# Hashed attention before a gated feed-forward block: the first batch's hash products taken pair by pair over four column groups, and its order of work rewritten

## The chip, the cores and the metric

The kernel runs on one core of a Trainium2 chip. The metric is device time in microseconds (us), the median of three runs: 339.31 us before the change (339.14 to 339.33). One more execution, taken with the hardware profiler, lasted 338.95 us; the span of its instructions, from the first to the last, is 337.2 us, and 1.75 us lie around it.

Engines are named as in the profile: PE is the matrix engine (PEld its weight loads), DVE the vector engine, ACT the activation engine, POOL the general engine, SP the engine that issues most transfers. Each works through its own list of instructions in order, and waits on semaphores where data come from another.

## The reference, cut to what matters

```python
q_bits = (einsum('bhsd,dk->bhsk', q, proj) > 0)     # 6 bits per token and head
k_bits = (einsum('bhsd,dk->bhsk', k, proj) > 0)
mask   = q_bucket[:, :, :, None] == k_bucket[:, :, None, :]
scores = where(mask, scale * q @ k.T, -1e9)
attn   = softmax(scores) @ v                        # batch 4, heads 8, 768 tokens, 64 dims
x      = attn, heads side by side                   # 3072 x 512
out    = x + sigmoid(x @ w_res) * ((gelu(x @ w_gate) * (x @ w_val)) @ w_out)
```

A token attends only to the tokens of its head whose six sign bits (a hash by `proj`) are the same. Everything that arrives is float32.

## The kernel before

**Pairs and batches.** Two heads form a pair; pairs 0 to 3 are batch 0, pairs 4 to 7 batch 1, and so on to pair 15. A tile that belongs to "(p, 0)" is of the q side of pair p, "(p, 1)" of its k side. The 768 tokens of a head lie on 128 partitions, six to a partition, so a pair's q has 12 blocks of 64 (`HT` = 12, `T` = 6).

**From q and k to scores.** `load` (L158) fetches one side of a pair, 384 KB, `load_v` (L166) its values; both are issued by SP and go through one queue, in order. `cast` writes q or k as bf16 into one of four tiles `nat`. `tr` (L270) turns the float32 blocks on DVE, 32x32 at a time, into `t32`. The hash product (L281) multiplies `t32` by `projw` in float32, two halves of the 64 dims summed, 32 output columns per job; up to four jobs stand side by side in four column groups of PE. DVE turns the sums back (`tokens`, L293), and `bits` (L302) writes the signs as six extra columns of `nat`, in four instructions of 32 partitions for a side, dealt out to DVE and POOL by a string such as 'vvvp'. With one more column of constants each token then has 71 columns, and one product of 71 rows gives the score and adds a large bonus for each equal bit. `turn` transposes `nat` on PE (L378) into PSUM and `copy` (L384 on ACT, L386 on DVE or POOL) brings it to `aug`; `turn_dma` (L364) does it by a transposing transfer instead, as for pair 3.

**Scores and values.** A pair has nine chunks. `S c` is chunk c of the batch (c = 0 to 35; pair 1 begins at S 9, pair 2 at S 18, pair 3 at S 27): PE fills 128x1024 scores into one of two PSUM buffers (L505), ACT takes the exponential (L516). `V c` multiplies the result by the values (L480). `vs` and `va` prepare the values of a pair on POOL (L391 to L403); `preset` adds a small share of `vs` to a head's sums on PE (L452, L455). `finish` (L424, L425) divides a head on DVE and writes `x_tok`; `xturn` (L464 to L469) or a transposing transfer (L433) makes `x_sb` of it, which the feed-forward products read.

**After the first batch.** `gate_val` multiplies `x_sb` by `wg` and `wv` (L530). Of its first step the parts of pairs 0 to 2 are done early (`gv` 0 and 1); the part of pair 3 waits for `finish` (3, 1) and `xturn` 3. Then come the hash products of pairs 6 and 7, which need `tr` (6, *) and `tr` (7, *). The later batches interleave scores with the feed-forward products of the batch before; their order comes from the lists in the kernel's body and isn't touched.

**What sets the order.** For batch 0 the order is written out by hand: `PLAN` (L17 to L73) is a list of steps, and each step puts its instructions at the end of its engine's list. Only the order within an engine counts; a load that stands late in PLAN is issued as soon as SP has come through what stands ahead of it. `('w',)` lets POOL issue the next piece of the weights (L245, 384 KB for each piece of `wg` and `wv`); the first two pieces stand in PLAN, seven more follow without a wait behind POOL's last step of PLAN. Buffers also order the work: four for each side's loads, three for `load_v`, one for the PSUM tile "r" (hash sums, and some `turn`s), one for the turned hash `ht`.

Before the change pair 1 is hashed by itself, both sides in two column groups (`hash (1,)`, eight matmuls), pairs 2 and 3 together in four (`hash (2, 3)`, sixteen matmuls).

## Time and profile before

| what | value |
|---|---|
| median of three runs | 339.31 us |
| the profiled execution, its span | 338.95 us, 337.2 us |
| PE busy | 331.5 us (98%) |
| DVE, ACT, POOL busy | 217.0, 213.3, 175.4 us |
| mean granted PE clock | 0.998 |
| bytes moved | 43.88 MB, 130 GB/s over the span |
| S 0 starts on PE, the last exponential of batch 0 starts on ACT | 7.70 us, 44.36 us |
| first product of the feed-forward block starts | 45.90 us |

A timeline row gives the start, the duration of the group, the engine, the line, the operation, the tiles (out<-in) with their shapes and the number of instructions merged into the row; in brackets stands the idle time just before, with what ended it. "PE busy" counts a matmul to its modelled end, so that consecutive rows of PE overlap a little; the chain of waits, where one piece begins when the one before ends, gives the time a group takes out of the sequence. A landing is counted from a transfer's issue to its semaphore.

### The profile page before, as it was taken

Reading aid. Unit: us, or ns where it says so; the run is one execution under the profiler, and the core shown is the slowest. Engines: PE = TensorE matmul, PEld = TensorE weight load, DVE = VectorE, ACT = ScalarE, POOL = GpSimd, SP = SyncE. Lnnn points to the kernel's source line nnn. Section 1 sums busy time; section 2 is a strip of 40 time slices with the busy share of each in tenths; the row PEclk is TensorE's granted clock in tenths of the full one; section 3 lists DMA queues with packets and bytes.
Section 4 is the critical chain, followed back from the end, with each engine's and each line's share of the span. In section 5 each row is a group of like instructions: output and inputs, shape, how many; then the busy total and the mean of one; then the engine's idle time right before and its main releaser. Section 6 shows DMA issues by size and latency. Waiting matters only on the chain.

```text
span 337.2 us, 7848 instructions
## 1 busy us (share of the span) xinstructions
PE 331.5 (98%) x3138; PEld 202.7 (60%) x3138; DVE 217.0 (64%) x461; ACT 213.3 (63%) x246; POOL 175.4 (52%) x261
## 2 busy tenths in 40 slices
PE   7999999999999999999999999999999999999996
PEld 6667666565666655655666665666566665666444
DVE  7887675664577958875687896876567444343243
...
GB/s 231 373 286 132 222 237 182 187 159 232 287 204 177 62 95 78 107 36 98 92 108 272 303 77 92 135 49 62 35 124 33 80 103 31 33 0 0 33 62 94
DMA packets 74387, 43.88 MB, mean 130 GB/s; under 512 B 52544, under 2 KB 71360, under 8 KB 74352
## 3 DMA queue, kind: packets, MB, share of 16 engines
q1 hardware_dynamic: 67872, 37.95, 44.4%
...
HBM read 29.56 MB, written 6.29 MB: 106 GB/s over the span
## 4 chain that ended last, share of the span: by engine, by line
PE 93%; ACT 3%; DVE 2%; issue 1%; DVEq 0%; ACTq 0%
PE sp L530 37%; PE fps L576 18%; PE sp L505 17%; PE av L480 9%; PE rps L562 6%; PE hs L281 3%; ACT ering L516 3%; PE wps L226 1%; ACT e L516 1%; PE hs L319 1%; PE pt L378 1%; PE pt L464 0%; DVE nat L329 0%; DVE o L582 0%; DVE aug L386 0%
## 5 line engine op out<-in xcount | busy, mean ns | idle before, releaser
L516 ACT ACTIVATE e<-sp 128x1024 bf16<-128x1024 f32 x117 | 117.7, 1028 | 8.3 <-PE sp L505 3.2
L339 POOL TENSOR_TENSOR pr<-ld,projr 128x384 f32<-128x384 f32 x96 | 93.8, 998 | 48.2 <-DVE sums L345 29.0
L547 ACT ACTIVATE gt<-sp 128x768 bf16<-128x768 f32 x48 | 38.9, 810 | 83.5 <-PE sp L530 77.9
L505 PE MATMUL sp<-aug,aug 71*128 71x256 bf16 (+1 forms) x384 | 86.2, 326 | 0.4
L576 PE MATMUL fps<-wo,hh 128*128 128x512 bf16 (+2 forms) x312 | 79.6, 363 | 0.0
L550 DVE TENSOR_TENSOR hh<-gt,sp 128x768 bf16<-128x768 bf16 x48 | 45.8, 954 | 44.2 <-PE sp L530 40.8
L530 PE MATMUL sp<-x_sb,wv 128*128 128x512 bf16 (+1 forms) x384 | 70.9, 326 | 0.0
L530 PE MATMUL sp<-x_sb,wg 128*128 128x512 bf16 (+1 forms) x384 | 70.9, 326 | 0.0
L480 PEld LDWEIGHTS <-e 128*128 128x128 bf16 x936 | 43.5, 97 | 25.9
L345 DVE TENSOR_REDUCE sums<-pr 128x6 f32<-128x384 f32 x96 | 50.0, 541 | 11.6 <-POOL pr L339 11.0
L530 PEld LDWEIGHTS <-wg 128*128 128x128 bf16 x384 | 37.0, 98 | 25.6 <-issue 1.2
L530 PEld LDWEIGHTS <-wv 128*128 128x128 bf16 x384 | 37.4, 98 | 25.0 <-issue 0.2
L480 PE MATMUL av<-va,e 128*128 128x65 bf16 x936 | 47.1, 193 | 0.0
L576 PEld LDWEIGHTS <-hh 128*128 128x128 bf16 x312 | 28.1, 97 | 22.0 <-issue 0.2
L505 PEld LDWEIGHTS <-aug 71*128 71x128 bf16 x384 | 29.0, 97 | 11.5 <-issue 2.0
L579 DVE SCALAR_TENSOR_TENSOR fps<-th,fps 128x512 f32<-128x512 f32 (+2 forms) x26 | 17.0, 652 | 26.2 <-PE fps L576 26.0
L516 ACT ACTIVATE ering<-sp 128x1024 bf16<-128x1024 f32 x27 | 25.9, 1031 | 3.0 <-PE sp L505 3.0
L562 PE MATMUL rps<-wr,x_sb 128*128 128x512 bf16 x96 | 27.1, 379 | 0.0
L566 ACT ACTIVATE th<-rps 128x512 f32<-128x512 f32 x24 | 14.3, 594 | 18.5 <-PE rps L562 18.5
L270 DVE STREAM_TRANSPOSE t<-ld 128x768 f32<-128x768 f32 (+3 forms) x28 | 22.9, 841 | 0.8 <-PE hs L281 0.6
L459 DVE COPY av<-av 128x390 f32<-128x390 f32 x24 | 13.5, 563 | 11.9 <-PE av L455 11.7
L260 POOL TENSOR_SCALAR nat<-ld 128x768 bf16<-128x768 f32 (+1 forms) x12 | 9.6, 804 | 17.7 <-DMA aug<-nat 16.8
...
## 6 DMA issues: line engine op xcount, KB each, us to landing
...
```

The source lines that it names most:

```text
L270: nc.vector.transpose(t32[p, side][:, sl].rearrange("p c h n -> p (c h n)"), raw[p, side][:, sl].rearrange("p c d -> p (c d)"))
L339: nc.gpsimd.tensor_mul(pr, raw[x][:, hi * T:(hi + 1) * T], projr[:, bit].unsqueeze(1).to_broadcast([P, T, D]))
L345: nc.vector.reduce_sum(sums[x][:, hi * T:(hi + 1) * T, bit], pr, axis=mybir.AxisListType.X)
L480: nc.tensor.matmul(av[p, hi][:, qt, :], e[:, off:off + P], va[:, hi, jt, 0:D + 1], start=first, stop=(repeats(p, hi) and jt == T - 1), ski ...
L505: nc.tensor.matmul(sp[:, off:off + nq * P], ks[0:KA, hi * T + jt, :], qs[0:KA, hi * T + qt0:hi * T + qt0 + nq, :], start=True, stop=True)
L516: nc.scalar.activation(e, sp, AF.Exp, scale=float(ALPHA))
L530: nc.tensor.matmul(sp[:, c0:c1], w[:, kk, bass.ts(m, P)], xs[:, kk, c0:c1], start=(kk == 0), stop=(kk == KM - 1))
L547: nc.scalar.activation(gt, sp[:, 0:S], AF.Gelu)
L550: nc.vector.tensor_mul(hidden[b][:, m, :], gt, ps[1][:, 0:S])
L562: nc.tensor.matmul(rps, x_sb[b][:, kk, t, :], wr[:, kk, :], start=(kk == 0), stop=(kk == KM - 1))
L576: nc.tensor.matmul(fps[:, cs], hh[:, m, bass.ts(t, P)], wo[:, m, cs], start=(m == 0), stop=(m == KF - 1))
L579: nc.vector.scalar_tensor_tensor(fps[:, cs], th[:, cs], 1.0, fps[:, cs], op0=ALU.add, op1=ALU.mult)
```

## The change: what it does

Three helpers are new. `hash_heads` puts the four halves of one pair (head 0 and 1 of q and k) into the four column groups: four matmuls for one half of the dims, eight for a pair, so 24 for pairs 1 to 3, as many as before. `head_tokens` turns the 192 columns of sums that come out, laid down in three parts; `head_bits` writes the bits of one head of one side in four instructions, so that 48 instructions of half the size take the place of 24.

PLAN is rewritten as a whole, with the same loads, casts, scores and values. What moves, beside the hash steps: the first piece of the weights (from S 6 to the head of the plan) and the second (from S 23 to S 32, behind `vs` 2, `va` 3, `vs` 4 and `vs` 3 on POOL); `load_v` 2 on SP from behind `load (3, 0)` to behind `load (4, 0)`; `load (6, 1)` from S 13 to S 24, `load (7, 0)` from S 26 to S 32 and `load (7, 1)` from S 21 to the very end of SP's list; `tr (7, 1)` on DVE from behind `finish (3, 1)` to ahead of it, and `tr (7, 0)` the other way. Of the `copy` steps, (0, 1) blocks 2 to 6, (0, 0) blocks 6 to 12 and (1, 0) blocks 6 to 12 go from DVE to ACT, (0, 0) blocks 4 to 6 and (0, 1) blocks 6 to 8 from ACT to DVE. `hash (4, 5)` 2 and 3 stand together at S 30.

```diff
--- before.py
+++ after.py
@@ -15,61 +15,63 @@
 
 
 PLAN = [
-    ('load', 1, 0), ('load', 1, 1), ('load_v', 0), ('load', 2, 0), ('load_v', 1), ('load', 2, 1),
-    ('load', 3, 0), ('load_v', 2), ('load', 3, 1), ('proj', 's', 'pssp'), ('cast', 0, 1, 'p', 0, 6),
-    ('proj', 'w', 'pppp'), ('cast', 0, 0, 'p', 6, 12), ('cast', 0, 0, 's', 0, 6), ('cast', 0, 1, 'p', 6, 12),
-    ('tr', 0, 0, 0, 4), ('tr', 0, 1, 0, 2), ('tr', 0, 0, 4, 6), ('tr', 0, 1, 2, 6), ('fill', 32, 114),
-    ('hash1', 0, (0, 0, 4, 'av'), (1, 0, 2, 'av')), ('hash1', 0, (0, 4, 6, 'w0'), (1, 2, 6, 'w1')),
-    ('bits1', 0, 0, 0, 4), ('bits1', 0, 1, 0, 2), ('bits1', 0, 0, 4, 6), ('bits1', 0, 1, 2, 6),
-    ('turn', 0, 1, 0, 2, 'f'), ('copy', 0, 1, 0, 2, 's'), ('turn', 0, 0, 0, 4, 'r'), ('copy', 0, 0, 0, 4, 's'),
-    ('turn', 0, 0, 4, 6, 'av'), ('copy', 0, 0, 4, 6, 's'), ('turn', 0, 1, 2, 6, 'f'),
-    ('tr', 0, 0, 6, 12), ('copy', 0, 1, 2, 6, 'v'), ('tr', 0, 1, 6, 12),
-    ('cast', 1, 0, 'p'), ('cast', 1, 1, 'p'), ('va', 0), ('load', 5, 0),
+    ('load', 1, 0), ('proj', 's', 'pssp'), ('load_v', 0), ('load', 1, 1), ('tr', 0, 0, 0, 4), ('tr', 0, 1, 0, 2),
+    ('fill', 32, 114), ('load', 2, 0), ('load', 2, 1), ('cast', 0, 0, 's', 0, 6), ('w',), ('tr', 0, 1, 2, 6),
+    ('tr', 0, 0, 4, 6), ('hash1', 0, (0, 0, 4, 'av'), (1, 0, 2, 'av')), ('cast', 0, 1, 'p', 0, 6),
+    ('proj', 'w', 'pppp'), ('hash1', 0, (0, 4, 6, 'w0'), (1, 2, 6, 'w1')), ('cast', 0, 1, 'p', 6, 12),
+    ('cast', 0, 0, 'p', 6, 12), ('load_v', 1), ('bits1', 0, 0, 0, 4), ('bits1', 0, 0, 4, 6), ('load', 3, 0),
+    ('load', 5, 0), ('turn', 0, 0, 0, 4, 'r'), ('bits1', 0, 1, 0, 2), ('turn', 0, 1, 0, 2, 'f'),
+    ('copy', 0, 0, 0, 4, 's'), ('turn', 0, 0, 4, 6, 'av'), ('bits1', 0, 1, 2, 6), ('copy', 0, 1, 0, 2, 's'),
+    ('turn', 0, 1, 2, 6, 'f'), ('copy', 0, 0, 4, 6, 'v'), ('cast', 1, 0, 'p'), ('copy', 0, 1, 2, 6, 's'),
+    ('load', 3, 1), ('load', 4, 0), ('load_v', 2), ('load', 5, 1), ('load', 4, 1),
     ('S', 0),
-    ('S', 1), ('hash1', 0, (0, 6, 12, 'av'), (1, 6, 12, 'av')), ('tr', 1, 0), ('bits1', 0, 0, 6, 12), ('bits1', 0, 1, 6, 12),
-    ('vs', 0), ('load', 4, 0), ('load', 5, 1), ('load', 4, 1), ('load_v', 3),
-    ('S', 2), ('turn', 0, 0, 6, 12, 'av'), ('tr', 1, 1), ('copy', 0, 0, 6, 12, 'v'),
-    ('S', 3), ('turn', 0, 1, 6, 12, 'f'), ('hash', (1,), 2), ('hash', (1,), 3), ('hash', (1,), 0), ('hash', (1,), 1),
-    ('copy', 0, 1, 6, 8, 's'), ('copy', 0, 1, 8, 12, 'v'), ('tokens', (1,)),
-    ('S', 4), ('V', 0), ('bits', 1, 0, 'v'), ('V', 1),
-    ('S', 5), ('bits', 1, 1, 'vvvp'), ('V', 2), ('vs', 1), ('V', 3),
-    ('S', 6), ('w',), ('turn', 1, 0, 0, 6, 'r'), ('copy', 1, 0, 0, 6, 'v'),
...
-    ('S', 12), ('hash', (2, 3), 2), ('hash', (2, 3), 3), ('copy', 1, 1, 6, 12, 'v'), ('cast', 2, 1, 'p'),
-    ('cast', 2, 0, 'p'), ('hash', (2, 3), 0), ('hash', (2, 3), 1), ('finish', 0, 0), ('tokens', (2, 3)),
-    ('bits', 2, 0, 'vvp'), ('bits', 2, 1, 'vp'),
-    ('S', 13), ('bits', 3, 1, 'vp'), ('V', 9), ('load', 6, 1),
...
-    ('S', 18), ('cast', 3, 1, 'p'), ('V', 14),
-    ('S', 19), ('bits', 3, 0, 'vvvp'), ('turn_dma', 3, 0), ('vs', 2), ('turn', 2, 1, 6, 12, 'f'),
-    ('turn', 2, 0, 6, 12, 'r'),
-    ('S', 20), ('turn_dma', 3, 1), ('load', 6, 0), ('V', 15), ('copy', 2, 0, 6, 12, 'v'), ('V', 16),
-    ('finish', 1, 0), ('copy', 2, 1, 6, 12, 'v'), ('tr', 4, 1),
-    ('S', 21), ('load', 7, 1), ('tr', 4, 0), ('vs', 4), ('load_v', 5), ('V', 17),
-    ('S', 22), ('V', 18), ('V', 19),
-    ('S', 23), ('w',), ('va', 3), ('V', 20), ('cast', 4, 0, 'p'), ('finish', 1, 1), ('cast', 5, 0, 'p'),
-    ('tr', 6, 1),
-    ('S', 24), ('V', 21),
-    ('S', 25), ('tr', 5, 1), ('V', 22),
-    ('S', 26), ('load', 7, 0), ('V', 23), ('V', 24), ('tr', 5, 0),
-    ('S', 27), ('V', 25),
-    ('S', 28), ('V', 26),
-    ('S', 29), ('hash', (4, 5), 2), ('finish', 2, 0),
-    ('S', 30), ('vs', 3), ('va', 4), ('V', 27), ('V', 28),
-    ('S', 31), ('hash', (4, 5), 3),
-    ('S', 32), ('V', 29), ('V', 30), ('tr', 6, 0), ('load_v', 6), ('finish', 2, 1),
-    ('S', 33), ('V', 31), ('finish', 3, 0),
-    ('S', 34), ('open', 4, 0), ('V', 32), ('xturn', 2),
-    ('S', 35), ('hash', (4, 5), 0), ('hash', (4, 5), 1), ('V', 33), ('tr', 7, 0), ('gelu',),
-    ('cast', 5, 1, 'p'), ('V', 34), ('V', 35), ('finish', 3, 1), ('gv', 0), ('tr', 7, 1), ('xturn', 3),
-    ('preset', 4, 0), ('tokens', (4, 5)), ('repeat', 4, 0), ('gv', 1), ('cast', 4, 1, 'p'),
+    ('S', 1), ('tr', 0, 0, 6, 12), ('tr', 0, 1, 6, 12), ('hash1', 0, (0, 6, 12, 'av'), (1, 6, 12, 'av')),
+    ('S', 2), ('va', 0), ('cast', 1, 1, 'p'), ('load_v', 3), ('tr', 1, 0), ('vs', 0), ('bits1', 0, 0, 6, 12),
+    ('bits1', 0, 1, 6, 12), ('turn', 0, 0, 6, 12, 'av'), ('copy', 0, 0, 6, 12, 's'),
+    ('S', 3), ('V', 0), ('turn', 0, 1, 6, 12, 'f'), ('copy', 0, 1, 6, 12, 'v'), ('V', 1), ('V', 2),
+    ('S', 4), ('tr', 1, 1),
+    ('S', 5), ('hash4', 1, 0), ('hash4', 1, 1), ('tr', 2, 0),
+    ('S', 6), ('tokens4', 1), ('bitsh', 1, 0, 0, 'pvvv'), ('V', 3),
+    ('S', 7), ('turn', 1, 0, 0, 6, 'r'), ('V', 4),
+    ('S', 8), ('bitsh', 1, 1, 0, 'vpvv'), ('turn', 1, 1, 0, 6, 'f'), ('copy', 1, 0, 0, 6, 'v'),
+    ('bitsh', 1, 0, 1, 'vpvp'), ('turn', 1, 0, 6, 12, 'r'), ('copy', 1, 0, 6, 12, 's'), ('copy', 1, 1, 0, 6, 'v'),
+    ('V', 5), ('bitsh', 1, 1, 1, 'ppvv'),
+    ('S', 9),
+    ('S', 10), ('vs', 1), ('cast', 3, 0, 'p'), ('va', 2), ('tr', 2, 1), ('turn', 1, 1, 6, 12, 'f'), ('hash4', 2, 0),
+    ('tr', 3, 0), ('va', 1), ('hash4', 2, 1), ('tr', 3, 1), ('copy', 1, 1, 6, 12, 'v'),
+    ('S', 11), ('cast', 2, 0, 'p'),
+    ('S', 12), ('load_v', 4), ('tokens4', 2), ('bitsh', 2, 0, 1, 'vvvv'), ('bitsh', 2, 1, 0, 'vpvp'),
+    ('cast', 2, 1, 'p'), ('V', 6), ('V', 7), ('V', 8), ('finish', 0, 0), ('bitsh', 2, 1, 1, 'pvvv'),
+    ('S', 13), ('hash4', 3, 0),
+    ('S', 14), ('hash4', 3, 1),
+    ('S', 15), ('bitsh', 2, 0, 0, 'vpvv'), ('tokens4', 3), ('V', 9),
+    ('S', 16), ('turn', 2, 1, 0, 6, 'f'), ('copy', 2, 1, 0, 6, 'v'), ('turn', 2, 0, 0, 6, 'r'),
+    ('copy', 2, 0, 0, 6, 'v'),
+    ('S', 17), ('V', 10),
+    ('S', 18), ('finish', 0, 1), ('V', 11), ('V', 12), ('cast', 3, 1, 'p'), ('bitsh', 3, 0, 0, 'vvvp'),
+    ('bitsh', 3, 0, 1, 'pppv'), ('turn_dma', 3, 0),
+    ('S', 19), ('bitsh', 3, 1, 1, 'vvvp'), ('bitsh', 3, 1, 0, 'vpvv'), ('V', 13),
+    ('S', 20), ('turn', 2, 1, 6, 12, 'f'), ('copy', 2, 1, 6, 12, 'v'), ('turn', 2, 0, 6, 12, 'r'), ('vs', 2),
+    ('va', 3), ('copy', 2, 0, 6, 12, 'v'),
+    ('S', 21), ('turn_dma', 3, 1), ('load', 6, 0), ('tr', 4, 1), ('V', 14), ('V', 15),
+    ('S', 22), ('V', 16),
+    ('S', 23), ('finish', 1, 0), ('V', 17),
+    ('S', 24), ('vs', 4), ('V', 18), ('tr', 5, 1), ('load', 6, 1), ('V', 19),
+    ('S', 25), ('V', 20), ('finish', 1, 1), ('V', 21),
+    ('S', 26), ('V', 22),
+    ('S', 27), ('V', 23), ('V', 24),
+    ('S', 28), ('V', 25), ('tr', 4, 0), ('V', 26),
+    ('S', 29), ('tr', 5, 0), ('vs', 3), ('finish', 2, 0),
+    ('S', 30), ('hash', (4, 5), 2), ('hash', (4, 5), 3),
+    ('S', 31),
+    ('S', 32), ('V', 27), ('load', 7, 0), ('load_v', 5), ('tr', 6, 1), ('V', 28), ('V', 29), ('w',), ('V', 30),
+    ('finish', 2, 1),
+    ('S', 33), ('V', 31), ('cast', 5, 1, 'p'),
+    ('S', 34), ('tr', 6, 0), ('finish', 3, 0), ('V', 32), ('xturn', 2),
+    ('S', 35), ('cast', 4, 1, 'p'), ('load_v', 6), ('hash', (4, 5), 0), ('hash', (4, 5), 1), ('V', 33), ('V', 34),
+    ('V', 35), ('cast', 5, 0, 'p'), ('load', 7, 1), ('tr', 7, 1), ('gv', 0), ('open', 4, 0), ('preset', 4, 0),
+    ('finish', 3, 1), ('tr', 7, 0), ('gelu',), ('va', 4), ('xturn', 3), ('tokens', (4, 5)), ('cast', 4, 0, 'p'),
+    ('gv', 1), ('repeat', 4, 0),
 ]
 BESIDE = [('hash', (6, 7), 0), ('hash', (6, 7), 1), ('hash', (6, 7), 2), ('hash', (6, 7), 3)]
 REPEATED = ()
@@ -282,6 +284,32 @@
                                      t32[x][:, sl, dh, :], start=(dh == 0), stop=(dh == 1),
                                      tile_position=(0, 32 * j))
 
+    def hash_heads(p, dh):
+        if dh == 0:
+            hsum[p] = ps_tile()
+        for g in range(4):
+            hi, side = divmod(g, 2)
+            nc.tensor.matmul(hsum[p][32 * g:32 * g + 32], projw[:, dh, :],
+                             t32[p, side][:, hi * T:(hi + 1) * T, dh, :], start=(dh == 0), stop=(dh == 1),
+                             tile_position=(0, 32 * g))
+
+    def ps_tile():
+        return mm_ps.tile([P, T, 32], FP32, tag="r", name="hs")
+
+    def head_tokens(p):
+        ht = hh_pool.tile([P, 3, HT // 3 + 1, 32], FP32, tag="ht", name="ht")[:, :, 0:T // 3]
+        nc.vector.transpose(ht.rearrange("p a c n -> p a (c n)"),
+                            hsum[p].rearrange("p (a c) n -> p a (c n)", a=3))
+        htok[p] = ht
+
+    def head_bits(p, side, hi, engs):
+        for a in range(4):
+            g = 32 * (2 * hi + side)
+            engs[a % len(engs)].tensor_scalar(
+                nat_of((p, side))[32 * a:32 * a + 32, hi * T:(hi + 1) * T, D:D + NBITS],
+                htok[p][g:g + 32, ..., NBITS * a:NBITS * (a + 1)], 0.0, 0.5,
+                op0=ALU.is_gt, op1=ALU.subtract)
+
     def hash_tok(jobs, psum=False):
         n = 32 * len(jobs)
         if psum:
@@ -715,7 +743,8 @@
             (lambda a: projw[32 * a:32 * a + 32, :, NBITS * a:NBITS * (a + 1)]),
             [ENG[e] for e in engs]),
         cast=lambda p, side, e, *c: cast(p, side, ENG[e], *c),
-        hash1=hash_runs,
+        hash1=hash_runs, hash4=hash_heads, tokens4=head_tokens,
+        bitsh=lambda p, side, hi, e: head_bits(p, side, hi, [ENG[x] for x in e]),
         bits1=bits_one,
         turn=lambda p, side, c0, c1, tag: turn_pe(p, side, c0, c1, tag, POOLS[tag]),
         copy=lambda p, side, c0, c1, e: turned(p, side, c0, c1, ENG[e]),
```

9 rows, old and new, of the table PLAN are left out of this document.

## The prediction

> **What bounds the kernel now.** I read the page first, then the chain of waits over the first batch, then ACT's timeline there. PE is the engine to watch, but a busy share over the whole span hides that one stretch has a second limit.
>
> ```profile
> span 337.2 us, 7848 instructions
> PE 331.5 (98%) x3138; PEld 202.7 (60%) x3138; DVE 217.0 (64%) x461; ACT 213.3 (63%) x246; POOL 175.4 (52%) x261
> ```
>
> From 46 us on PE runs the feed-forward products and the later batches without a gap, and nothing of that is edited. The change is worth what it does to the time until then. ACT's timeline of that part:
>
> ```profile
> 8.33 1.94 ACT L516 ACTIVATE ering<-sp 128x1024 bf16<-128x1024 f32 x2 [0.50 <-PE sp L505]
> 10.45 2.00 ACT L516 ACTIVATE ering<-sp 128x1024 bf16<-128x1024 f32 x2 [0.18 <-PE sp L505]
> 12.35 0.37 ACT L384 ACTIVATE aug<-pt 71x256 bf16<-71x256 bf16 x1
> 14.06 4.84 ACT L516 ACTIVATE ering<-sp 128x1024 bf16<-128x1024 f32 x5 [1.34 <-PE sp L505]
> 23.78 8.62 ACT L516 ACTIVATE ering<-sp 128x1024 bf16<-128x1024 f32 x9 [0.95 <-PE sp L505]
> 44.36 1.02 ACT L516 ACTIVATE e<-sp 128x1024 bf16<-128x1024 f32 x1
> ```
>
> ACT starts at 8.33, waits for scores 0.18, 1.34 and 0.95 us, and from 23.78 to 45.38 takes 23 exponentials with no wait, 0.94 to 0.96 us each (8.62 / 9). The two large waits stand beside the two hash blocks of pairs 1 to 3. So the first batch ends by ACT, and by PE wherever a hash block stops it from feeding ACT.
>
> **The change, part by part: PE.** The chain of waits gives what each hash block (L281) takes out of PE's sequence:
>
> ```profile
> 11.73 1.75 PE hs L281 x16
> 21.70 1.44 PE hs L281 x32
> 38.55 0.46 PE hs L281 x8
> 44.26 0.79 PE hs L281 x16
> ```
>
> The first two are pair 1 in two column groups (eight matmuls, 16 records) and pairs 2 and 3 in four. The other two are pairs 4 and 5 in four groups: half a pair's work in 0.46, twice that in 0.79. After the change pairs 1 and 2 are blocks of the 0.79 kind and pair 3 two of 0.46: 2.50 in place of 3.19. `hash (4, 5)` 2 and 3, now together, cost 0.79 in place of 2 x 0.46. PE saves 0.69 + 0.13 = 0.8 us, and no block is longer than 0.79, which is less than one exponential.
>
> **ACT and the bits.** Of 128-column blocks ACT now copies 22 in five instructions where it had 10 in four. By these rows a column costs (582 - 375) / 256 = 0.81 ns and an instruction 168 ns, so ACT gets 1536 x 0.81 + 168 = 1.4 us more; against that stand the 2.47 us of waits that can go. The best end for ACT is thus 1.1 us earlier, with every wait gone.
>
> ```profile
> L384 ACT ACTIVATE aug<-pt 71x256 bf16<-71x256 bf16 x3 | 1.1, 375 | 2.5 <-PE pt L378 2.5
> L384 ACT ACTIVATE aug<-pt 71x512 bf16<-71x512 bf16 x1 | 0.6, 582 | 0.0
> L386 DVE COPY aug<-pt 71x768 bf16<-71x768 bf16 x9 | 4.8, 540 | 2.5 <-PE pt L378 2.5
> L302 DVE TENSOR_SCALAR nat<-ht 32x72 bf16<-32x72 f32 x17 | 3.7, 218 | 0.3
> L302 POOL TENSOR_SCALAR nat<-ht 32x72 bf16<-32x72 f32 x7 | 3.2, 456 | 3.8 <-DVE ht L293 3.5
> L329 DVE TENSOR_SCALAR nat<-hs 128x36 bf16<-128x36 f32 x1 | 0.2, 196 | 0.0
> ```
>
> A bit instruction of 36 elements isn't in the trace for 32 partitions; on DVE it lies between the 196 of the 128x36 row and the 218 of 32x72, and I take 0.19; on POOL half of 456 and the whole of it are the ends, I take 0.38. DVE goes from 17 x 0.218 = 3.7 to 32 x 0.19 = 6.1 us, POOL from 7 x 0.456 = 3.2 to 16 x 0.38 = 6.1.
>
> Walking the order with these durations I get the fifth exponential at 13.45 (before: 14.06), since PE puts V 0 to V 2 and not a hash block ahead of S 4; the tenth no earlier than before, because ACT has then paid for both large copies; the fourteenth at 22.95 (before: 23.78), as PE has no block of 1.44 there. Some 0.4 us are given back between S 30 and S 35, where 0.79 and then four V chunks stand together. With every load in time the first batch gains 0.5 us.
>
> **The loads at the start.** They aren't in time. The queue of SP is full from 2.7 us to 19 us, and the trace shows what a piece of the weights does to it:
>
> ```profile
> 12.00:18.00 6.00, 6.00 (x89) 4.57 (x87) 4.77 (x13) 4.63 (x7) 4.33 (x10) 1.00 1.06 373
> q0 software_dynamic: 2669, 2.01, 130.7%
> L158 SPq DMA_DIRECT2D ld<-in_q_dram x1: 368/368/368, 10.0 to 10.0; - x1
> DMA to landing us min/median/max: 9.7/9.7/9.7
> 17.84 0.83 POOL L391 CAST va<-ldv 128x768 bf16<-128x768 f32 x1
> 14.81 1.00 POOL L399 TENSOR_TENSOR v<-ldv 128x384 f32<-128x384 f32 x1
> ```
>
> From 12 to 18 us the loads alone move 373 GB/s, 1.05 us for 384 KB. The second row is the weights' queue from 46 to 56 us, alone: 2.01 MB in 10 us, so 1.95 us for a piece of 384 KB. The third and fourth are the load of (4, 0), the 13th tile in SP's order: issued at 10.0, landed at 19.7. After the change the 13th is `load_v` 2, and a piece of weights goes ahead in the full queue. It lands at 19.7 plus 1.05 (by bytes) to 1.95 (by the weights' own rate): 20.7 to 21.7. POOL comes to `va` 2 after `vs` 1 (17.84 - 14.81 - 0.97 of weights = 2.06) and a cast: at 18.4 to 19.7. It waits 1 to 3 us, and behind it stand `va` 1, the casts of pair 2 and its last four pieces of bits.
>
> Who waits for POOL: turn (2, 1) on PE needs the cast, the turned hash of pair 3 needs POOL's last read of `ht`, and turn (2, 0) needs that, all ahead of S 17 on PE. From the start of `va` 2 it is two values 1.8, two casts 1.6, four bit pieces 1.5, the turn on DVE 0.4, turn and S 17 with their delays 1.1: 6.5 us, so the exponential of S 17 starts at 27.2 to 28.2. Before it starts at 23.78 + 4 x 0.96 = 27.6. The gain is eaten: -0.4 to +0.6 at this point, and I carry nothing.
>
> **The loads at the end.** Here I expect the loss. SP's list before, and its last landing:
>
> ```profile
> 21.44 0.37 SPq L158 DMA_DIRECT2D ld<-in_k_dram  x1
> 28.04 3.17 SPq L364 DMA_TRANSPOSE aug<-nat  x2
> 31.26 0.96 SPq L158 DMA_DIRECT2D ld<-in_q_dram  x1
> 34.12 1.31 SPq L433 DMA_TRANSPOSE x_sb<-x_tok  x1
> 36.51 0.37 SPq L166 DMA_DIRECT2D ldv<-in_v_dram  x1
> DMA to landing us min/median/max: 7.9/7.9/7.9
> ```
>
> (6, 1) went at 21.44, when the queue was free. Between the two transposing transfers of pair 3 and the end stood five loads, and the last, `load_v` 6, landed at 36.51 + 7.9 = 44.4, needed by nobody for long. After the change (6, 1) is one of six, and the last of the six is (7, 1). That adds 1.05. The transfers of pair 3 also start later: behind the turned hash at 25.8 to 26.8 DVE has two copies (1.1), `finish` (0.7) and ten bit pieces (1.9), so the second goes at 30.0 to 31.0, 0.5 to 1.5 after the 29.5 of before; I take 1.0. (7, 1) lands at 44.4 + 1.05 + 1.0 = 46.4.
>
> Who needs it: `tr (7, 1)`, now ahead of `finish (3, 1)` on DVE.
>
> ```profile
> 46.10 0.20 DVE L424 RECIPROCAL rec<-av 128x6 f32<-128x6 f32 x1
> 46.80 0.97 DVE L270 STREAM_TRANSPOSE t<-ld 128x768 f32<-128x768 f32 x1
> 47.91 0.42 DVE L467 COPY x_sb<-pt 128x512 bf16<-128x512 bf16 x1
> 46.94 0.51 PE L464 MATMUL pt<-ident,x_tok 128*128 128x128 bf16 x6
> 48.38 0.49 PE L530 MATMUL sp<-x_sb,wg 128*128 128x512 bf16 x2
> ```
>
> Before, `finish (3, 1)` starts at 46.10, PE turns its result at 46.94, and the last part of the first feed-forward step starts at 48.38; one `tr` stands between `finish` and the copy then and after, so that stretch keeps its length. After, `finish` starts at 46.4 + 0.97 = 47.4, 1.3 us later. PE has nothing else: `gv` 0 is done at about 46.5, and preset, `xturn` 3 and `gv` 1 are queued behind.
>
> **The weights beside the loads.** POOL's train of seven weight pieces starts after its last cast, and a train beside SP's queue slows that queue:
>
> ```profile
> 39.87 0.83 POOL L245 DMA_DIRECT2D wg<-in_moe_w_gate_dram  x1
> 32.18 0.85 POOL L245 DMA_DIRECT2D wv<-in_moe_w_val_dram  x1
> DMA to landing us min/median/max: 9.4/9.4/9.4
> q0 software_dynamic: 164, 0.13, 91.3%
> q1 hardware_dynamic: 49, 0.07, 22.9%
> ```
>
> Between 36 and 37 us, beside the piece issued at 32.18, the loads (q1) got 70 GB/s of the 373. The train's issue moves from 39.87 by POOL's delay, 0 to 2 us. If it moves the first bytes while 1 us of loads is outstanding, these take 373 / 70 = 5.3 us and (7, 1) comes 4.3 us later; if the train is late by as much as the loads, nothing. Between 0 and 4.3 I take 0.3, near the end that before shows, where `load_v` 6 still came through 4.5 us after the train's first issue. The Trainium skill, DMA: Bandwidth & Descriptors, section Queues, rings and completion order, says that each DMA engine takes turns between its queues packet by packet; the row has 164 packets against 49, so this case's trace does not bear out equal turns; by that rule the loads would get 106 packets of 1.4 KB in that 1 us, 152 GB/s, and an outstanding 1 us would cost 1.5 and not 4.3.
>
> The second piece of weights itself moves from 32.18 (landed 9.4 us after, the third row) to between 35 and 37 us, so it lands at 44.4 to 46.4; `gv` 1 reads it at about 48, so the wait for pair 3 covers it. Without that cover it is due at 46.9 and has 0.5 us to spare.
>
> **The sum.** Hash on PE -0.8 and ACT's waits less its copies, together -0.5; POOL's wait for `load_v` 2 takes that back; (7, 1) late +1.3; the train +0.3. The profiled execution goes from 338.95 to 340.55; the median of runs stands 0.36 above it, so 339.31 + 1.6 = 340.9.
>
> **Rivals.** *The order holds* (faster): (7, 1) lands by 44.6, because the queue before had slack that I count as work, and `load_v` 2 arrives with POOL. For it: no engine but POOL has more to do than it has time for. Against it: both queue rows. It gives -0.5, at best -1.1: 338.2 to 338.8. *It cancels*: (7, 1) lands between 44.6 and 45.7, and the loss is what was gained: 338.7 to 339.9. *The train starves the last load* (slower still): 1 us of loads outstanding when it starts, +4.3 on top of +1.3 less what is shared: 343 to 345. *The early piece of weights delays `load (1, 0)`*, behind which DVE holds the bits of pair 0: +0.3 to +1, part of every case above.
>
> **How the numbers follow.** Late (7, 1), 340.0 to 343: 0.44. Starved: 0.13. Cancels: 0.24. Order holds: 0.19. A measurement of this kernel can tell about 0.2% (0.68 us) from no change. Slower by more: 0.44 + 0.13, say 0.57; within: 0.24; faster by more: 0.19. The range for 8 in 10 is 338.6 to 343.7; the forecast's own is 340.0 to 343.
>
> **What would show it.** On DVE a transpose (L270) that waits for a load of k just ahead of the last `finish`, and on PE a gap between `gv` 0 and `xturn` 3 at 46 to 48 us. On POOL a wait of 1 to 3 us at `va` (L391) for a load of v near 20 us. On ACT no wait beside a hash block, but one near 27 us. Hash blocks of 0.79 and 0.46. I am wrong if L530 starts its eight-matmul rows earlier than before, or if the 0.8 us of PE show up as such.

## The result and the profile after

The changed kernel takes 342.25 us (median of six runs, 341.6 to 346.88), the kernel before 339.28 on the same chips; the ratio is 1.0082, 95% interval 1.0059 to 1.0105. The change makes the kernel slower, by 2.8 us going by the ratio and 3.0 between the medians. The run of 346.88, in the slow state at a mean granted PE clock of 0.988, counts in the median and not in the ratio. The profiled execution lasted 341.75 us with a span of 340.0, so 2.8 over the 338.95 and 337.2 of before.

The page of the kernel after, its span and busy times:

```profile
span 340.0 us, 7831 instructions
PE 329.4 (97%) x3091; PEld 202.6 (60%) x3138; DVE 218.2 (64%) x475; ACT 214.9 (63%) x247; POOL 177.5 (52%) x270
```

DVE's timeline at the end of the first batch (start, duration, engine, line, operation, tiles; in brackets the idle time before and what ended it), where before had the reciprocal at 46.10:

```profile
47.52 0.98 DVE L272 STREAM_TRANSPOSE t<-ld 128x768 f32<-128x768 f32 x1 [2.82 <-DMA ld<-in_k_dram]
...
48.53 0.15 DVE L452 RECIPROCAL rec<-av 128x6 f32<-128x6 f32 x1
```

L272 is `tr`, L452 `finish`. `tr (7, 1)` waits 2.82 us for its load, and `finish (3, 1)` behind it starts at 48.53, 2.43 us later than before. From there on the two kernels keep that distance: the reciprocal of the second batch that started at 92.23 starts 2.4 us later too, and so does DVE's last computing step (336.88, 334.47 before). So 2.4 of the 2.8 us are made here; the remaining 0.4 stands behind that last step. The chain of waits says which transfer it is (its hash blocks, L292, are shown for later), and PE's timeline what it costs:

```profile
13.77 0.86 PE hs L292 x16
...
19.53 0.90 PE hs L292 x16
...
22.74 0.46 PE hs L292 x8
...
23.74 0.46 PE hs L292 x8
...
38.09 9.34 DMA ld<-in_k_dram
47.52 0.99 DVE t L272
```

```profile
46.18 1.14 PE L558 MATMUL sp<-x_sb,wg 128*128 128x512 bf16 x6
48.67 0.19 PE L483 MATMUL av<-vsum,eps_sb 128*128 128x65 bf16 x1 [1.36 <-DVE rec L452]
49.33 0.51 PE L492 MATMUL pt<-ident,x_tok 128*128 128x128 bf16 x6 [0.46 <-DVE x_tok L453]
...
50.77 0.48 PE L558 MATMUL sp<-x_sb,wg 128*128 128x512 bf16 x2
```

`load (7, 1)` goes out at 38.09 and lands 9.34 us later, at 47.43. PE has nothing between `gv` 0 (46.18) and the preset (48.67), and the last part of the first step starts at 50.77 where it was 48.38.

ACT's timeline of the first batch, beside the one that the prediction shows of before:

```profile
13.32 4.91 ACT L544 ACTIVATE ering<-sp 128x1024 bf16<-128x1024 f32 x5 [0.20 <-PE sp L533]
18.13 0.80 ACT L412 ACTIVATE aug<-pt 71x768 bf16<-71x768 bf16 x1
18.82 1.93 ACT L544 ACTIVATE e<-sp 128x1024 bf16<-128x1024 f32 x2
21.01 1.94 ACT L544 ACTIVATE e<-sp 128x1024 bf16<-128x1024 f32 x2 [0.26 <-PE sp L533]
22.84 3.94 ACT L544 ACTIVATE ering<-sp 128x1024 bf16<-128x1024 f32 x4
27.34 4.81 ACT L544 ACTIVATE ering<-sp 128x1024 bf16<-128x1024 f32 x5 [0.56 <-PE sp L533]
...
40.94 3.77 ACT L544 ACTIVATE ering<-sp 128x1024 bf16<-128x1024 f32 x4 [0.43 <-PE sp L533]
44.64 1.02 ACT L544 ACTIVATE e<-sp 128x1024 bf16<-128x1024 f32 x1
```

The waits of 1.34 and 0.95 beside the hash blocks are gone; 0.20 and 0.26 (at 13.32 and 21.01) are left there. A new one stands at 27.34 (the exponential of S 17) and one at 40.94, and the last exponential starts at 44.64, 0.28 after that of before. Before, `finish (3, 1)` started 0.72 us behind the end of the last exponential (46.10, 45.38), and the same distance stands in the three experiments whose `finish` doesn't wait for the load and whose times are compared below (46.50, 47.09 and 45.68). By it `finish` could have started at 46.38 here. So of its 2.43 us some 2.15 are the load's and 0.28 ACT's. POOL's rows at the bits of pair 1 and at `va` 2 show what is late ahead of S 17:

```profile
15.16 2.35 POOL L308 TENSOR_SCALAR nat<-ht 32x36 bf16<-32x36 f32 x6 [2.19 <-DVE ht L301]
...
20.89 0.82 POOL L419 CAST va<-ldv 128x768 bf16<-128x768 f32 x1 [0.39 <-DMA ld<-in_k_dram]
```

The second row names a load of k as what ended the wait; `va` reads only `ldv`, and `load_v` 2, issued at 10.3, landed 10.5 us later, at 20.83.

### The profile page after: what moved, and what is told of

The parts are those of the page before. It is cut to its first block, busy times and chain, and to the rows that moved or that the text cites. A ratio compares the mean times of both kernels' runs of the same rounds, so it can differ in the third digit from the quotient of the medians.

```text
span 340.0 us, 7831 instructions
## 1 busy us (share of the span) xinstructions
PE 329.4 (97%) x3091; PEld 202.6 (60%) x3138; DVE 218.2 (64%) x475; ACT 214.9 (63%) x247; POOL 177.5 (52%) x270
## 3 DMA queue, kind: packets, MB, share of 16 engines
q0 software_dynamic: 6400, 5.44, 10.5%
## 4 chain that ended last, share of the span: by engine, by line
PE 89%; DVE 4%; DMA 3%; issue 1%; POOL 1%; SPq 0%; ACT 0%; DVEq 0%
PE sp L558 36%; PE fps L604 17%; PE sp L533 16%; PE av L508 9%; PE rps L590 6%; DMA ld<-in_k_dram 3%; DVE t L272 1%; PE pt L406 1%; PE hs L283 1%; PE wps L228 1%; POOL pr L367 1%; PE hs L292 1%; DVE sums L373 1%; PE hs L347 1%; DVE x_tok L453 0%
## 5 line engine op out<-in xcount | busy, mean ns | idle before, releaser
L604 PE MATMUL fps<-wo,hh 128*128 128x512 bf16 (+2 forms) x287 | 74.4, 361 | 1.3
L590 PE MATMUL rps<-wr,x_sb 128*128 128x512 bf16 x91 | 26.0, 379 | 0.2
L272 DVE STREAM_TRANSPOSE t<-ld 128x768 f32<-128x768 f32 (+3 forms) x28 | 22.9, 842 | 5.0 <-DMA ld<-in_k_dram 4.7
## 6 DMA issues: line engine op xcount, KB each, us to landing
wv<-in_moe_w_val_dram POOLq DMA_DIRECT2D x4, 384.0 KB, 10.2
```

Source lines behind the costliest of these rows:

```text
L272: nc.vector.transpose(t32[p, side][:, sl].rearrange("p c h n -> p (c h n)"), raw[p, side][:, sl].rearrange("p c d -> p (c d)"))
L590: nc.tensor.matmul(rps, x_sb[b][:, kk, t, :], wr[:, kk, :], start=(kk == 0), stop=(kk == KM - 1))
L604: nc.tensor.matmul(fps[:, cs], hh[:, m, bass.ts(t, P)], wo[:, m, cs], start=(m == 0), stop=(m == KF - 1))
```

## The experiments

The theory after the result: the loss is `tr (7, 1)` ahead of `finish (3, 1)`, with its load at the end of SP's list and beside the train of weights; what the new order gains up to then is taken back by POOL, which comes late to the bits of pair 2. Rivals: the new form of the hash, or the order as a whole, costs time elsewhere. All times below are medians; each ratio is to the kernel before on the same chip. "Finish" is the start of the reciprocal of `finish (3, 1)` in the profiled execution, 46.10 before and 48.53 after.

**The load of (7, 1) further ahead.** In the kernel after, SP issues it right behind (6, 1).

```diff
-    ... ('tr', 5, 1), ('load', 6, 1), ('V', 19),
+    ... ('tr', 5, 1), ('load', 6, 1), ('load', 7, 1), ('V', 19),
...
-    ... ('cast', 5, 0, 'p'), ('load', 7, 1), ('tr', 7, 1),
+    ... ('cast', 5, 0, 'p'), ('tr', 7, 1),
```

> The changed kernel, with one load moved: SP issues the load of (7, 1) right behind that of (6, 1), ahead of the transposing transfer of pair 1's result, of (7, 0) and of the values of pairs 5 and 6. Theory (the transpose of (7, 1) on DVE waits for the last load of SP's list): DVE's wait of 2.82 us there goes, finish (3, 1) starts at about 46.4 and not 48.5, and the kernel takes 2.1 to 2.4 us less than the changed one, 339.7 to 340.1. Rival (the time was lost earlier, by POOL and ACT, and the wait only shows it): under 0.5 us less, 341.8 or more.

340.33 us (339.16 to 343.89), ratio 1.0039, 1.0007 to 1.0071. DVE's timeline of that kernel, ACT's and POOL's:

```profile
45.47 0.98 DVE L272 STREAM_TRANSPOSE t<-ld 128x768 f32<-128x768 f32 x1 [0.65 <-PE hs L283]
...
46.50 0.20 DVE L452 RECIPROCAL rec<-av 128x6 f32<-128x6 f32 x1
```

```profile
27.46 4.81 ACT L544 ACTIVATE ering<-sp 128x1024 bf16<-128x1024 f32 x5 [1.04 <-PE sp L533]
```

```profile
21.01 0.82 POOL L419 CAST va<-ldv 128x768 bf16<-128x768 f32 x1 [0.88 <-DMA ld<-in_k_dram]
```

`tr (7, 1)` no longer waits for its load, and finish comes 2.03 us earlier with one transfer moved. 1.9 us of the 3.0 in the medians are gone, or 1.5 of the 2.8 by the ratios, a little less than the 2.1 to 2.4 expected; the two intervals still overlap, so the proof lies in the trace and in the next experiment. That the load's place, ahead of this `tr`, is the main cause is shown by the two together. What is left, 0.40 us at finish, goes with ACT, whose wait near 27 us is 1.04 here.

**Only the transpose moved.** DVE takes `tr (7, 1)` behind `xturn` 3; the load stays last.

```diff
-    ... ('load', 7, 1), ('tr', 7, 1), ('gv', 0), ...
+    ... ('load', 7, 1), ('gv', 0), ...
...
-    ... ('xturn', 3), ('tokens', (4, 5)), ...
+    ... ('xturn', 3), ('tr', 7, 1), ('tokens', (4, 5)), ...
```

> The changed kernel, all loads as they are; only DVE's list differs: the transpose of (7, 1) stands behind finish (3, 1), the transpose of (7, 0) and the copy of xturn 3. If the late load hurts only because finish (3, 1) is queued behind it, the load still lands at about 47.4 and the time falls by 1.7 to 2.4 us, to 339.8 to 340.6; the hash products of pairs 6 and 7 then wait for it by 0 to 0.7 us. If the loss is elsewhere, the time stays at 341.8 or above.

340.95 us (340.09 to 342.24), ratio 1.0029, 1.0002 to 1.0057: below the interval of the kernel after, though short of the fall that was expected. Finish is at 47.09, and in front of it stands PE and no load:

```profile
47.09 0.20 DVE L452 RECIPROCAL rec<-av 128x6 f32<-128x6 f32 x1 [1.55 <-PE av L480]
...
49.24 0.97 DVE L272 STREAM_TRANSPOSE t<-ld 128x768 f32<-128x768 f32 x1
```

The late load by itself does no harm here; it costs because DVE, which takes its list in order, has `finish` behind it. Finish is 0.59 us later than in the kernel of the last experiment because ACT is, 0.27 of it by a longer wait for S 17 (1.31 at 28.05).

**The train of weights later.** Eight fills of a scratch tile on POOL put the train's first issue from 40.99 to 43.53.

```diff
-    ('gv', 1), ('repeat', 4, 0),
+    ('gv', 1), ('repeat', 4, 0), ('idle', 8),
```

> The changed kernel, with eight memsets of a scratch tile on POOL (2.5 to 3.5 us in all) ahead of the seven weight pieces that follow POOL's last step of the first batch. If the weights' train slows the last load by the 1.1 us that its landing (2.13 us after the one before, where others of this size are 1.05 apart) suggests, the load of (7, 1) lands at 46.2 to 46.5 and the time falls by 0.9 to 1.2 us. If the queue of SP is late by itself, the time stays within 0.3 us.

341.95 us (340.31 to 345.2), ratio 1.008, 1.0045 to 1.0116, which the kernel after has as well: in the time the expected fall of 0.9 to 1.2 us did not come. The wait goes from 2.82 to 2.54:

```profile
46.95 0.98 DVE L273 STREAM_TRANSPOSE t<-ld 128x768 f32<-128x768 f32 x1 [2.54 <-DMA ld<-in_k_dram]
```

The load landed 1.25 us behind `load_v` 6 instead of 2.13, so the gap in front of the last landing does follow the train. The other profiles say the same: the last load of SP's list, whichever it is, lands 1.94 to 2.47 us behind the one before it in the other ten of the new order, and 1.03 to 1.24 behind it in the three of the old order. But here the load landed 9.37 us after its own issue, as against 9.34, since the loads ahead of it were later too: the second piece of the weights landed at 45.23 instead of 44.24 and may have lain longer beside them. What the train alone costs in the end time is not resolved.

**The same order of loads in the kernel before.** (6, 1) goes where (7, 1) went, (7, 1) goes last, and DVE turns it ahead of `finish (3, 1)`; everything else, the hash too, is as before.

```diff
-    ('S', 13), ('bits', 3, 1, 'vp'), ('V', 9), ('load', 6, 1),
+    ('S', 13), ('bits', 3, 1, 'vp'), ('V', 9),
...
-    ('S', 21), ('load', 7, 1), ('tr', 4, 0), ...
+    ('S', 21), ('load', 6, 1), ('tr', 4, 0), ...
...
-    ... ('tr', 6, 0), ('load_v', 6), ...
+    ... ('tr', 6, 1), ('tr', 6, 0), ('load_v', 6), ('load', 7, 1), ...
...
-    ... ('V', 33), ('tr', 7, 0), ... ('gv', 0), ('tr', 7, 1), ('xturn', 3),
+    ... ('V', 33), ('tr', 7, 1), ... ('gv', 0), ('tr', 7, 0), ('xturn', 3),
```

> The kernel before, with its own hash steps and order; only three loads and three transposes of the end are put as in the changed kernel: load (6, 1) goes where (7, 1) was, load (7, 1) to the end of SP's list, the transpose of (6, 1) to S 32, that of (7, 1) ahead of finish (3, 1) and that of (7, 0) behind it. If the order of the loads is the cause by itself, this kernel is 1.0 to 2.5 us slower than the one before, 340.3 to 341.8, with DVE waiting for a load of k just ahead of the last finish. If the cause needs the new hash steps or the new bits, it stays within 0.5 us of the kernel before.

339.74 us (339.33 to 343.15), ratio 1.0026, 0.9999 to 1.0053.

```profile
45.22 0.98 DVE L269 STREAM_TRANSPOSE t<-ld 128x768 f32<-128x768 f32 x1 [0.94 <-DMA ld<-in_k_dram]
46.13 0.16 DVE L423 RECIPROCAL rec<-av 128x6 f32<-128x6 f32 x1
```

This is the outcome of the second case: the time stays within some 0.5 us. DVE does wait for the load, 0.94 us, but it lands at 45.13 and finish is at 46.13, where it was. The order of loads by itself costs nothing at finish, and no loss that is clear of noise. It takes the other 2.3 us of lateness (47.43 - 45.13) to cost something: 1.24 of them are the later issue (38.09, here 36.85), 1.06 the longer way from issue to landing (9.34, here 8.28). After the change SP's transposing transfers of pair 3 go out 1.5 us later (29.54 for the first, 28.04 before), and the train stands beside the last load.

**The load ahead, and POOL's list mended.** Beside the first experiment's edit POOL casts pair 2 first and takes `va` 1 and `va` 2 later.

```diff
-    ('S', 10), ('vs', 1), ('cast', 3, 0, 'p'), ('va', 2), ... ('va', 1), ...
-    ('S', 11), ('cast', 2, 0, 'p'),
+    ('S', 10), ('vs', 1), ('cast', 3, 0, 'p'), ...
+    ('S', 11), ('cast', 2, 0, 'p'), ('cast', 2, 1, 'p'), ('va', 1),
...
-    ... ('bitsh', 2, 0, 0, 'vpvv'), ('tokens4', 3), ...
+    ... ('bitsh', 2, 0, 0, 'vpvv'), ('va', 2), ('tokens4', 3), ...
```

> The changed kernel with the load of (7, 1) moved as in the first experiment, and with POOL's list rearranged at one place: the casts of (2, 0) and (2, 1) come right behind that of (3, 0), then va 1, then the bit pieces of pair 2, and va 2 only behind them. Theory (ACT's wait near 27 us comes from POOL, which does va 2 and va 1 ahead of what the turned hash of pair 3 needs): that wait, 0.56 to 1.31 us in four profiles, falls under 0.3; the two transposing transfers of pair 3 are issued 0.5 to 1.2 us earlier; the time falls by 0.4 to 1.0 us from the first experiment's, to about the kernel before or 0.5 under it (338.8 to 339.6). Rival (DVE or PE set that wait): no difference to the first experiment beyond 0.2 us.

339.05 us (338.67 to 343.15), ratio 1.0009, 0.9983 to 1.0035. ACT runs from S 13 to S 21 without a wait, and finish is at 45.68:

```profile
22.73 8.72 ACT L544 ACTIVATE ering<-sp 128x1024 bf16<-128x1024 f32 x9
...
43.94 1.02 ACT L544 ACTIVATE e<-sp 128x1024 bf16<-128x1024 f32 x1
```

So both losses are named and both can be taken out, and the first batch then ends 0.42 us before that of the kernel before, near the 0.5 that the prediction gave the change with every load in time. The interval does not show it. Eight of the twelve executions took 338.67 to 339.11, with a median of 338.99; at such clocks the kernel before had 339.31 on this chip, with some of its runs as low. The other four took 340.23 to 343.15 and are those with a mean granted PE clock of 0.995 or less. The profile fell on the longest, and PE's timeline of it shows a wait far behind the first batch:

```profile
86.72 0.50 PE L604 MATMUL fps<-wo,hh 128*128 128x512 bf16 x1 [2.58 <-DMA wo<-in_moe_w_out_dram]
```

**POOL's list alone.** The kernel after with only that half of the edit.

> The changed kernel with POOL's list rearranged as in the run beside it, but with its own order of loads. If the late transfers of pair 3 carry into the landing of (7, 1), that load lands 0.5 to 1.2 us earlier (46.2 to 46.9 and not 47.4), and the time falls by as much, to 340.6 to 341.6. If the landing is set by the weights and the order of loads alone, it stays at 47.2 to 47.6 and the time within 0.3 us.

342.47 us (340.91 to 345.74), ratio 1.0101, 1.0057 to 1.0146. ACT's wait near 27 us is gone, DVE's is not (3.58 us). Nothing can be said of the difference to the kernel after, since four of its six executions had a mean clock of 0.995 or less, and in the profiled one the clock was 0.50 from 10 to 12 us (shown at the end). Whether the late transfers of pair 3 carry into the landing of (7, 1) stays open.

**Only the form of the hash.** The kernel before, its order and its loads, with pairs 1 to 3 hashed by the new helpers; `turn (2, 0)` stands one slot later, for the tile "r".

```diff
-    ... ('hash', (1,), 2), ('hash', (1,), 3), ('hash', (1,), 0), ('hash', (1,), 1), ... ('tokens', (1,)),
+    ... ('hash4', 1, 0), ('hash4', 1, 1), ... ('tokens4', 1),
...
-    ('S', 13), ('bits', 3, 1, 'vp'), ('V', 9), ...
+    ('S', 13), ('hash4', 3, 0), ('hash4', 3, 1), ('tokens4', 3), ('bitsh', 3, 1, 0, 'vp'), ('bitsh', 3, 1, 1, 'vp'), ...
```

> The kernel before, with its own order, loads and weights; only pairs 1 to 3 are hashed one by one with the new helpers in the places of the old steps (bits dealt out as 'v' and 'vvvp'; the products of pair 3 stand behind S 13, since the one buffer for hash sums must be free, and the turn of (2, 0) one slot later for the same reason). Theory: PE's 0.7 us are saved, but ACT has waits of 0.2 to 0.8 in place of 1.34 and 0.95 and the bits cost DVE and POOL 3 us each: 338.6 to 339.6, the kernel before within 0.6. If the new form itself costs the time, it is over 0.7 us slower, above 340.

339.87 us (339.5 to 341.25), ratio 1.0015, 0.9996 to 1.0034: above the 338.6 to 339.6 expected, under the 340 of the other case. Two waits of ACT beside hash blocks became six:

```profile
13.56 4.84 ACT L542 ACTIVATE ering<-sp 128x1024 bf16<-128x1024 f32 x5 [0.70 <-PE sp L531]
19.11 3.89 ACT L542 ACTIVATE e<-sp 128x1024 bf16<-128x1024 f32 x4 [0.71 <-PE sp L531]
...
24.98 1.94 ACT L542 ACTIVATE ering<-sp 128x1024 bf16<-128x1024 f32 x2 [0.65 <-PE sp L531]
```

The sum of all six is 2.85 against the 1.34 + 0.95 of before, and finish is 0.73 us later. Shorter hash blocks are no gain by themselves. Why is only argued: pair 3 now has its own turn through the one PSUM tile "r" and the one `ht`, and it takes the new order to keep that out of ACT's way.

**The other cure for POOL's wait.** The load ahead as in the first experiment, and `load_v` 2 in its old place behind `load (3, 0)`.

> The changed kernel with the load of (7, 1) moved as in the first experiment, and with load_v 2 two places further ahead in SP's list, behind load (3, 0), where the kernel before has it. If the late landing of load_v 2 is what stops POOL, POOL's wait ahead of va 2 (0.4 to 1.1 us) goes, ACT's wait near 27 us falls by 0.3 to 0.9 and the time by as much from the first experiment's. If POOL's list is too full in any case, ACT still waits 0.3 us or more there.

339.96 us (339.09 to 343.04), ratio 1.0021, 0.9998 to 1.0044. POOL's wait at `va` 2 and ACT's near 27 us are both gone in the profile. But that execution is one whose clock fell to 0.59 from 8 to 12 us: POOL comes to `va` 2 only at 21.44, when the load of the kernel after would have been there too (20.83), and ACT starts S 13 at 23.82, 0.98 later than there. So the profile alone does not show that the wait came from this load. The times speak for it: the seven executions with a mean clock above 0.995 have a median of 339.30, the seven of the first experiment 339.92. In the kernel with the load ahead and POOL's list mended, whose first batch ran at a clock of 1.00, ACT's wait is gone too, there by POOL's order.

**Work for PE in the gaps at the start.** To the kernel with both cures (the load ahead and POOL's list mended) six matmuls of constants are added, two behind the first hash, two behind each of the first two turns.

> e5_load71_pool with six more 128x114 matmuls of constants on PE, two behind the last piece of the first hash, two behind the first turn, two behind the second, each 0.10 us by the row of the 32 that are there (3.20 / 32). Theory: the runs of the new order in which the granted clock falls below 1 between 8 and 12 us (about 22 of 66 executions had a mean clock of 0.995 or less, against 9 of 82 of kernels with the order of before) come from PE being idle 0.7 to 1.2 us between 4 and 8 us; with 0.6 us of that filled they are as rare as before: at most 2 of 12 with a mean clock of 0.995 or less, median 338.9 to 339.1, and the first batch unchanged (last exponential ends 44.9 to 45.1). Rival: the clock falls for another cause (what PE does between 8 and 12 us, or the chip), then 3 to 6 of 12 again and a median of 339.0 to 339.5.

341.62 us (341.21 to 341.88), ratio 1.0073, 1.0061 to 1.0085: a miss. No execution had a clock under 0.999, but the next experiment, without filler on the same chip, had none below 0.998 either, so the theory of the clock isn't tested. The time went otherwise:

```profile
8.01 0.41 PE L411 MATMUL pt<-ident,nat 128*71 128x128 bf16 x4 [0.72 <-DVE nat L362]
...
207.60 0.48 PE L563 MATMUL sp<-x_sb,wg 128*128 128x512 bf16 x2 [1.41 <-DMA x_sb<-x_tok]
```

The sums of (0, 1) blocks 2 to 6 lie in the tile that the filler writes, and their turn comes at 8.01 (7.65 after). Finish is 1.26 us later than without filler (46.94, 45.68): 0.51 of it is there at the fifth exponential (13.72, 13.21), the rest comes with a wait of ACT for scores at 37.18, which is not explained. And a transposing transfer was late in a later batch.

**The two halves of `hash (4, 5)` apart.** The kernel with both cures, and

```diff
-    ('S', 30), ('hash', (4, 5), 2), ('hash', (4, 5), 3),
-    ('S', 31),
-    ('S', 32), ('V', 27), ...
+    ('S', 30), ('hash', (4, 5), 2),
+    ('S', 31), ('hash', (4, 5), 3), ('V', 27),
+    ('S', 32), ...
```

> e5_load71_pool with the two halves of hash (4, 5) apart again, one behind S 30 and one behind S 31, and V 27 ahead of S 32. Theory: the block of 0.86 us and the four V chunks behind S 32 are what makes ACT wait 0.42 us at 40 us; with both spread that wait goes, the last exponential ends near 44.55 instead of 44.96 and the median is 338.65, 0.6 to 0.7 us under before. Rival: the wait moves to the next block, S 35's, or finish (3, 1) is bound by something else by then: 339.0 as e5.

339.59 us (338.63 to 342.16), ratio 1.0027, 1.0005 to 1.0048. ACT's timeline from S 26 on:

```profile
35.03 9.03 ACT L544 ACTIVATE ering<-sp 128x1024 bf16<-128x1024 f32 x9
43.98 1.02 ACT L544 ACTIVATE e<-sp 128x1024 bf16<-128x1024 f32 x1
```

The wait of 0.42 at 40 us is gone as one piece, but nothing is gained: the nine exponentials take 9.03 us (8.52 for the same nine before), and the last one starts at 43.98 and ends at 45.00, 0.04 later than without the split. So the block was not what held ACT up, or something else holds it as much; the forecast of 44.55 for its end failed, and the rival's 339.0 is nearer. Of twelve executions six took 338.63 to 339.17 and six 340.01 to 342.16, all at a mean clock of 0.998 or more. The profiled one took 341.53 although finish was at 45.72, 0.38 before that of the kernel before. SP's timeline, of the kernel before and then of this one, shows where it went:

```profile
71.22 11.63 SPq L364 DMA_TRANSPOSE aug<-nat  x4
82.91 0.99 SPq L158 DMA_DIRECT2D ld<-in_q_dram  x1
```

```profile
70.85 17.80 SPq L392 DMA_TRANSPOSE aug<-nat  x4
88.70 1.46 SPq L160 DMA_DIRECT2D ld<-in_q_dram  x1
```

The four transposing transfers of pairs 6 and 7 hold SP's list for 17.80 us instead of 11.63, and the next batch's first load goes out 5.8 us later. DVE's rows at the same `finish`, before and then in this kernel, where it stands behind a sum of POOL's products of that load:

```profile
92.23 0.20 DVE L424 RECIPROCAL rec<-av 128x6 f32<-128x6 f32 x1 [0.76 <-PE av L480]
```

```profile
94.27 0.56 DVE L373 TENSOR_REDUCE sums<-pr 128x6 f32<-128x384 f32 x1 [3.64 <-POOL pr L367]
94.74 0.18 DVE L452 RECIPROCAL rec<-av 128x6 f32<-128x6 f32 x1
```

The same `finish` is 2.51 us later than before there, so far more is lost than the 0.38 that the first batch had gained.

**All of it, and a copy back on DVE.** Filler, split and `copy (1, 0)` blocks 6 to 12 on DVE.

> Both of the other two, and the copy of blocks 6 to 12 of (1, 0) on DVE instead of ACT, 0.54 instead of 0.81 us. Theory: ACT saves its 0.81 us at 18 us where it waits for nothing else, so the last exponential ends near 43.9, finish (3, 1) starts near 44.6 and the median is 338.0 to 338.3. Rival: ACT then waits for scores further on, because DVE comes to turn (2, *) later or PE can't feed it, and half or more is given back: 338.4 to 338.8.

343.39 us (342.61 to 346.52), ratio 1.0113, 1.0099 to 1.0128. The copy saves ACT 0.80 us and leaves it a wait of 1.47 in the same place, since DVE comes to it later:

```profile
20.06 1.94 ACT L549 ACTIVATE e<-sp 128x1024 bf16<-128x1024 f32 x2 [1.47 <-PE sp L538]
```

Finish is at 47.77, 2.09 later than with both cures alone; the filler by itself had cost 1.26 of that. Behind it come the late transfers near 85 us again. How the rest of the loss divides between them was not tested.

**The train earlier.** The kernel of the split, with two pieces of the train issued ahead of POOL's last casts.

```diff
-    ... ('V', 29), ('w',), ('V', 30),
+    ... ('V', 29), ('w',), ('w',), ('w',), ('V', 30),
...
-    (0, 'w'), (0, 'w'), (3, 'w'), ...
+    (3, 'w'), ...
```

> e10_split with two of the seven weight pieces of the train issued ahead of POOL's last five casts instead of behind them (right behind the second piece, near 36.4 us instead of 40.4 us). What it tells apart: e10's runs lie in two groups, 338.6 to 339.2 and 340.0 to 342.2, at the same clock. In its profile, one of the second group, the first batch ends 0.4 us before that of the kernel before, but the train's last piece lands at 60.5 us, 2.9 us after the first transposing transfer of the second batch is issued (before: 1.65), the third piece of the output weights lands at 83.9 (before: 78.9), and PE loses its time from 80 to 110 us. Theory: what the first batch gains is lost there, since the transposing transfers now meet the end of the train and crowd the output weights. With the train 1.5 to 2 us earlier the overlap is 0.9 to 1.4 us, the third piece lands near 78.5 and no execution is above 339.5; median 338.6 to 338.9, 0.2 to 0.5 us under before. Rival: the stall has another cause (the transfers' own spacing, or chance); the two groups stay, with 3 to 6 of 12 above 340 and a median near 339.3.

339.93 us (338.68 to 341.15), ratio 1.0005, 0.9983 to 1.0027: what the theory forecast did not come, and its condition did not either. In the profiled execution, whose clock was 0.62 from 8 to 12 us and whose first batch ended 1.1 us later for it, the train's last piece landed at 61.84, as against 60.53 in the kernel of the split: the pieces that went out first lay beside the loads of `v`, which landed 2.8 to 3.0 us later (47.66 and 49.60, against 44.68 and 46.79). The overlap with the transposing transfers was 3.06 us (2.89 with the split alone), and the executions are spread as before. In these runs the kernel before had four of sixteen at 341.15 to 341.26 too.

No version is shown to be faster than the kernel before. The best two are level with it.

## Why the prediction was right, and where a size was off

The forecast was 340.9, slower, in a range to 343.7; measured are 342.25. The case that came is the forecast's own, `load (7, 1)` late.

**PE.** Hash blocks of 0.86 and 0.90 for pairs 1 and 2 and twice 0.46 for pair 3 stand for the predicted 0.79 and 2 x 0.46, so 2.68 us in place of 2.50. That this would not show in the time held: ACT bounds that stretch, and the form alone, in the old order, made it longer.

**ACT and the bits.** The walk through the order gave 13.45, "no earlier" and 22.95 for the fifth, tenth and fourteenth exponential; they came at 13.32, 18.82 (18.95 before) and 22.84. The bits cost 181 ns on DVE and 329 on POOL, under the 190 and 380 assumed; the 0.19 us for DVE was also outside the working's own bounds of 196 and 218:

```profile
L308 DVE TENSOR_SCALAR nat<-ht 32x36 bf16<-32x36 f32 x32 | 5.8, 181 | 0.5
L308 POOL TENSOR_SCALAR nat<-ht 32x36 bf16<-32x36 f32 x16 | 5.3, 329 | 3.3 <-DVE ht L301 2.2
```

"With every load in time the first batch gains 0.5 us" is borne out in part: 0.42 with both cures, of which one rearranges POOL's list beside the load. With both loads ahead and POOL's list as it was, no profile at full clock exists, and the executions at a clock above 0.995 are level with the kernel before (339.30, 339.31).

**The loads at the start.** `load_v` 2 landed at 20.83, in the range of 20.7 to 21.7. POOL's wait was said to be 1 to 3 us and was 0.39 (0.88 and 1.14 in two experiments): POOL came to `va` 2 at 20.5 and not at 18.4 to 19.7, after a wait of 2.19 us for the turned hash of pair 1. The exponential of S 17 at 27.34 lies in the range given, and by the predicted way: 20.89 for the start of `va` 2 and the 6.5 us behind it (its parts add up to 6.4). "I carry nothing" was off by the 0.28 us that the last exponential came late.

**The loads at the end: the term that was mis-sized.** The working had 44.4 + 1.05 + 1.0 = 46.4 for the landing, and 0.3 for the train in the sum. What stands ahead of (7, 1) was right: `load_v` 6 landed at 45.29, where 44.4 + 1.0 makes 45.4, and the second transposing transfer went at 31.1, just past the 30.0 to 31.0 given. The load's own step took 2.13 us and not 1.05, with the train's first bytes at 45.0 and that load still to go. That term was too small: beside the train the last load took 1.1 us more, not 0.3, and the whole term is 2.43 at finish instead of 1.3 + 0.3. That the train is what lengthens this step rests on the ten gaps of 1.94 to 2.47 us against 1.25 with the train later; the time of that experiment did not show it. The remaining 0.4 of the 2.8 us is the end of the program, for which the sum had no term. The bytes of the two queues from 45 to 46 us:

```profile
q0 software_dynamic: 193, 0.15, 95.3%
q1 hardware_dynamic: 61, 0.08, 24.6%
```

The loads (q1) got some 80 GB/s, as the 70 of the row in the prediction. The Trainium skill, DMA: Bandwidth & Descriptors, section Queues, rings and completion order, has each DMA engine take turns between its queues by whole packets, each a group of some 9 to 17 descriptors. The prediction set the profile's packets against that rule, 164 to 49, and here they are 193 to 61. But these are pieces of 0.8 KB (0.15 MB / 193) and 1.3 KB, and no run shows that one of them is a packet in the page's sense; so the counts neither bear the rule out nor refute it, and the 106 packets and 152 GB/s that the prediction drew from it have no footing here.

**The weights.** The second piece landed at 44.24, a hair before the 44.4 to 46.4 given, and PE did not wait for it.

**The rivals.** "The order holds" and "it cancels" fell with the wait of 2.82. "Starved" (343 to 345) has the right mechanism at a fourth of its price. Of the early piece of weights no harm is seen: `load (1, 0)` landed at 7.06 (7.57 before), and the fifth exponential came at 13.32.
